# Second chunk through row loads and TensorE transposes, weights requested early, later casts held, rows loaded in pairs

## The chip, the cores and the metric

The kernel runs on one core of a Trainium2 chip. A core has a matrix engine (TensorE, PE in the profile), a vector engine (VectorE, DVE), an activation engine (ScalarE, ACT), a general engine (GpSimd, POOL) and a queue for DMA requests (SyncE, SP). Each of them works through its own instructions in order; they wait for each other through semaphores. The metric is the device time of one execution in microseconds (us).

## The reference

The reference is a short causal convolution followed by a two-layer network with a gated nonlinearity.

```python
# x: (8, 4096, 192), weight: (8 heads, 7 taps); each head has 24 channels
w = softmax(weight, axis=-1)                       # over the 7 taps
x_pad = 6 zero rows ahead of each sequence
out = einsum('hk,bskhg->bshg', w, windows_of_7(x_pad))   # per head, causal
# 32768 tokens of 192 channels; w_in: (192, 2048), w_out: (2048, 192), beta: (2048,)
h = out @ w_in
g = h * sigmoid(beta * h)
y = g @ w_out
```

All inputs and the result are float32; the kernel computes the network in bfloat16 with float32 sums.

## The kernel before, in words

**Tiling.** The eight sequences are folded into two halves, h = 0 and 1, so one chunk is 512 tokens of sequence p and of sequence p + 4 at once; there are 32 chunks. The 192 channels are cut into three groups of 64 (`NG`), so a chunk in transposed form, `xt`, is 128 partitions (half, channel within the group) by three groups by 16 + 512 tokens, the 16 in front being the halo of the tokens before (`HALO`).

**How a chunk is made.** For chunks 1 to 31, `cast(ch)` (line 97) issues two DMAs on POOL's queue, one for each half, that convert the rows to bfloat16 into a tensor `xd` in HBM. `xpose(ch)` (line 110) issues one transposing DMA on SP's queue that brings it into SBUF as `xt`. `conv_ops` (line 336) then makes the convolved chunk `ct` on VectorE, 21 operations for three groups and seven taps, with the softmaxed taps in `cw`. Chunk 0 goes another way, since nothing is there yet: its rows are loaded by SP (line 140), cast by VectorE (line 262), transposed by TensorE (line 270), copied out of PSUM by ScalarE (line 273), and convolved on TensorE with diagonal matrices (`diag_tap`, line 254). Those matrices hold the taps before they are normalized (`eu`), and the sums are scaled by `rn` on the way out (lines 305 and 307). Group 0 of chunk 1 is also convolved on TensorE, in the generator `conv1` (line 326), whose seven steps are spread over u = 4 to 10 of stage 0; it first converts the chunk's group 0 to `xt1` (line 327).

**Weights.** `w_in` is loaded in four quarters of 512 columns and held on both halves of the partitions. The first quarter is loaded twice by SP as float32 and cast by VectorE (lines 145 and 309); the other three are loaded and cast by DMAs on POOL's queue (`load_w_in`) into the lower half and copied to the upper half by VectorE (`copy_w_in`, line 186). `w_out` is loaded in four quarters by SP (`load_w_out`, line 132) and scaled by 1/beta on VectorE (`scale_w_out`, line 291). SP's order before is: the rows of chunk 0, w_in's first quarter, w_out's first quarter, the transpose of chunk 1, then the other w_out quarters.

**The main loop.** Stage s handles chunk s in 16 steps u. A step computes 128 of the 2048 hidden columns for all tokens of the chunk (`hidden`, line 355: six matmuls on 64 rows each, two of them side by side, into one of two PSUM tiles `ph`, then one activation on ScalarE into `g`). Beside it run output pairs (`output`, line 440). An output job covers 256 tokens (one half, two blocks of 128) and needs 32 pairs of matmuls, two for each of the 16 hidden column blocks; a stage has four jobs, so 128 pairs. Two jobs can be under way, in slots a and b, which are the PSUM tiles `pa` and `pb`. A pair can only run on hidden columns that are at least two steps old (`LAG`). `output(s, u, pairs, free)` runs up to `pairs` pairs, the oldest job first, and gives free slots named in `free` to waiting jobs. A job that ends is reduced by VectorE from its PSUM tile (line 412), and SP writes the result out. What is left after the last stage is drained in a closing loop.

**The order written out by hand.** VectorE's convolution operations stand in a queue, from which each step pops some: in stage 0 one or two a step from u = 4 on (16 in all), later 24 a stage. `first_work` gives the steps of stage 0 at which VectorE prepares further quarters of the weights. Every stage issues `cast(s + 4)` at u = 0 and `xpose(s + 2)` at u = 1, where the operations of chunk s + 2 also join the queue. Matmuls of zeros (`fill`, line 211) run between the first small matmuls.

Of the kernel before, what the change touches and what calls it, by code (L numbers as in the profile page):

```python
# [9 lines left out]
FP32 = mybir.dt.float32  # L10
FP32R = mybir.dt.float32r
BF16 = mybir.dt.bfloat16
# [5 lines left out]
def kernel(  # L18
# [17 lines left out]
    nc = tc.nc  # L36

    B, S, D = x.shape
# [3 lines left out]
    DG = 64  # L42
# [41 lines left out]
    def in_b():  # L84
        return psum_b.tile([128, 2, TOK], FP32, name="pb")
# [23 lines left out]

    def xpose(ch):  # L110
        r0 = HALO if ch % CHUNKS == 0 else 0
        xd = xds.pop(ch)
        nc.sync.dma_start_transpose(  # L113
            new_xt(ch)[:, :, r0:], xd[r0:].rearrange("t c h d -> t (c h d)")
        )
# [2 lines left out]
    NW = 4  # L118
    FW = F // NW
    NQ = NF // NW  # L120
    x0 = setup.tile([128, NB, 2, D], FP32)
    x0b = setup.tile([128, NB, NG, 2, DG], BF16)
    w_in_s = consts.tile([128, NG, F], BF16)
    w_in_raw = setup.tile([128, NG, FW], FP32)
    w_out_s = consts.tile([128, NF, D], BF16)
    w_out_raw = setup.tile([128, NF, D], FP32)
    w_in_v = moe_w_in.rearrange("(c d) f -> d c f", c=NG)
# [7 lines left out]
    cw8 = setup.tile([H, K], FP32)  # L135
    beta_q = setup.tile([NF, 128], FP32)
    nc.scalar.dma_start(out=cw8, in_=weight)
    nc.scalar.dma_start(out=beta_q, in_=moe_beta.rearrange("(c p) -> c p", p=128))
    for b in range(NB):
        nc.sync.dma_start(  # L140
            out=x0[:, b, :, :], in_=x_v[0, b * BLK : (b + 1) * BLK, :, :]
        )
    for r in range(2):
        nc.sync.dma_start(
            out=w_in_raw[r * DG : (r + 1) * DG], in_=w_in_v[:, :, 0:FW]
        )
    load_w_out(0)

    zeros = setup.tile([128, TOK], BF16)
    nc.vector.memset(zeros, 0.0)  # L150
# [29 lines left out]
    def load_w_in(i):  # L180
        cols = slice(i * FW, (i + 1) * FW)
        nc.gpsimd.dma_start(out=w_in_s[0:DG, :, cols], in_=w_in_v[:, :, cols])

    def copy_w_in(i):
        cols = slice(i * FW, (i + 1) * FW)
        nc.vector.tensor_copy(w_in_s[DG : 2 * DG, :, cols], w_in_s[0:DG, :, cols])

    cast(1)
    for i in range(1, NW):
        load_w_in(i)  # L190
    cast(2)
    cast(3)
    xpose(1)
    for i in range(1, NW):
        load_w_out(i)

    nmax = setup.tile([H, 1], FP32)
    nc.vector.reduce_max(nmax, cw8, axis=mybir.AxisListType.X, negate=True)
    nc.scalar.activation(
        e8[:, 0:K], cw8, AF.Exp, bias=nmax, accum_out=e8[:, K : K + 1]  # L200
    )
    nc.scalar.activation(warm, warm, AF.Silu)
    sel_r = setup.tile([H, NG, 2, DG], FP32R)
    nc.vector.tensor_copy(sel_r, sel)
# [14 lines left out]
    def spread(dst, sel, e8):  # L219
        for c in range(NG):  # L220
            nc.tensor.matmul(
                dst[:, c * (K + 1) : (c + 1) * (K + 1)],
                sel[:, c, :, :].rearrange("i h d -> i (h d)"),
                e8,
                start=True,
                stop=True,
            )

    fill(5)
    pc = in_a()  # L230
    spread(pc[:, 0, :], sel_r, e8r)
    fill(1, 384)
    eu = setup.tile([128, NG, K + 1], FP32)
    nc.vector.tensor_copy(eu.rearrange("p c k -> p (c k)"), pc[:, 0, 0:NK])

    diag = setup.tile([128, NG, K, 128], FP32R)

# [13 lines left out]
    def new_ct(s):  # L251
        cts[s] = ct_pool.tile([128, NG, TOK], BF16, name="ct")
# [4 lines left out]
            pv, diag[:, c, k, :], xt[:, o : o + TOK], start=(k == 0), stop=(k == K - 1)  # L257
        )


    for b in range(NB):
        nc.vector.tensor_copy(
            x0b[:, b].rearrange("q c h d -> q h c d"),
            x0[:, b].rearrange("q h (c d) -> q h c d", c=NG),
        )
    for b in range(NB):
        pool, name = (psum_b, "pb") if b % 2 == 0 else (psum_a, "pa")
        pt = pool.tile([128, NG, BLK], BF16, name=name)
        for c in range(NG):
            nc.tensor.transpose(  # L270
                pt[:, c, :], x0b[:, b, c].rearrange("q h d -> q (h d)"), ident_b
            )
        nc.scalar.copy(xt0[:, :, HALO + b * BLK : HALO + (b + 1) * BLK], pt)  # L273
        fill(1, 128)
    pb = pf[:, 1, 0:NF]
    nc.tensor.transpose(pb, beta_q, ident[0:NF, 0:NF])
    fill(1)
    diag_v(0)
# [10 lines left out]
    def scale_w_out(i):  # L289
        fcs = slice(i * NQ, (i + 1) * NQ)  # L290
        nc.vector.tensor_tensor(  # L291
            w_out_s[:, fcs, :],
            w_out_raw[:, fcs, :],
            beta_r[:, fcs].unsqueeze(2).to_broadcast((128, NQ, D)),
            ALU.mult,
        )

    new_ct(0)
    for c in range(NG):
        pv = psum_h.tile([128, 2, TOK], FP32, name="ph") if c < 2 else in_a()  # L300
        pv = pv[:, 0, :]
        for k in range(K):
            diag_tap(c, k, xt0[:, c], pv)
        if c < 2:
            nc.vector.tensor_scalar_mul(cts[0][:, c, :], pv, rn[:, c : c + 1])  # L305
# [9 lines left out]
    def taps():  # L315
# [5 lines left out]
        nc.vector.tensor_tensor(  # L321
            cw, pq[:, :, 0:K], rq.unsqueeze(2).to_broadcast((128, NG, K)), ALU.mult
        )


    def conv1():
        nc.vector.tensor_copy(xt1, xts[1][:, 0, :])  # L327
# [112 lines left out]
    def output(s, u, pairs, free):  # L440
        for _ in range(pairs):
            for name in free:
                if slots[name] is None and waiting:
                    slots[name] = waiting.popleft()

            live = [(j.s, j.h, j.q, n) for n, j in slots.items() if j is not None]
            for *_, name in sorted(live):
                job = slots[name]
                if job.ready(s, u):
                    break  # L450
            else:
                return
            if job.po is None:
                job.po = place[name]()
            if job.pair():
                job.leave()
                slots[name] = None

    conv1_work = conv1()
# [75 lines left out]
```

## Time and profile before

| what | us |
|---|---|
| median of ten runs | 719.84 (718.32 to 721.74) |
| the profiled execution, its own time | 718.32 |
| its span, first to last instruction | 716.6 |
| TensorE busy | 695.0 (97%) |
| ScalarE busy | 578.5 (81%) |
| VectorE busy | 522.2 (73%) |
| POOL busy | 60.3 (8%) |

A row of the profile names a line of the kernel, an engine, an operation and its tiles, written out<-in; then come the count, the busy time, the mean of one in ns, and the idle time of the engine just before it with what ended that. `PEld` is the loading of weights into TensorE, which overlaps its matmuls. A `q` behind an engine's name means its queue of requests, not its arithmetic. Rows of the timeline begin with the start and the length in us; several like instructions are merged into one row with their count. Rows of the chain of waits hold start, length, and what the end of the program waited for in that time. In the rows by stretch of time the number after the busy times is the clock that TensorE was granted, as a share of the full one.

### The profile page before, as it was taken

The page shows a single profiled execution, that of the slowest core. Times are in us where ns is not written, and L with a number is a line of the kernel's source. Part 1 is how long each engine was busy: PE and PEld are TensorE (multiplying, and loading weights), DVE is VectorE, ACT ScalarE, POOL GpSimd, SP SyncE. Part 2 cuts the span into 40 slices and gives each one's busy share as a digit, 9 for nine tenths or more (in the row PEclk, how much of TensorE's full clock was granted, in tenths as well). Part 3 has the DMA queues.
Part 4 walks back from the last instruction along what each step waited for, and adds up shares of the span by engine and source line. Part 5 has one row for each costly group of instructions (what it writes and reads, how often), then busy time and mean ns, then how long its engine had stood idle before and what let it go on. Part 6 is the DMA issues. An engine that isn't in the chain of part 4 may idle for free.

```text
span 716.6 us, 24619 instructions
## 1 busy us (share of the span) xinstructions
PE 695.0 (97%) x11325; PEld 521.2 (73%) x11325; DVE 522.2 (73%) x807; ACT 578.5 (81%) x532; POOL 60.3 (8%) x74
## 2 busy tenths in 40 slices
PE   8599999999999999999999999999999999999997
PEld 5267777777777777777777777777777777777776
DVE  5478887988977777977777987667887777797221
ACT  5388888888888888888888888888888888888883
POOL 6374442000000000000000000000000000000000
PEclk9799999999999999999999999999999999999999
DMA  9999999422123222132223122232112322213111
GB/s 184 184 164 165 169 176 171 78 57 60 32 69 69 58 68 57 36 57 68 58 68 59 46 48 69 62 64 57 50 42 70 68 57 59 61 38 63 46 40 52
DMA packets 188088, 55.57 MB, mean 78 GB/s; under 512 B 151168, under 2 KB 187600, under 8 KB 187984
## 3 DMA queue, kind: packets, MB, share of 16 engines
q0 software_dynamic: 99536, 13.13, 28.0%
q1 hardware_dynamic: 88400, 40.86, 24.3%
q8 instruction: 88, 1.44, 0.8%
q14 instruction: 16, 0.13, 0.1%
q10 hardware_dynamic: 48, 0.01, 0.0%
HBM read 29.40 MB, written 37.70 MB: 94 GB/s over the span
## 4 chain that ended last, share of the span: by engine, by line
PE 59%; DVE 24%; DMA 11%; issue 4%; SPq 1%; POOL 0%; ACT 0%; POOLq 0%; DVEq 0%
PE ph L363 28%; PE pa L393 16%; DVE ct L347 16%; PE pb L393 14%; DMA xt<-xd 8%; DVE osb L412 7%; DMA xd<-in_x_dram 2%; DMA w_out_raw<-in_moe_w_out_dram 1%; DVE ct L345 1%; SPq L420 1%; PE pb L256 1%; SPq L113 0%; ACT g L371 0%; POOL xd L104 0%; DVE w_out_s L291 0%
## 5 line engine op out<-in xcount | busy, mean ns | idle before, releaser
L371 ACT ACTIVATE g<-ph,beta 128x1024 bf16<-128x1024 f32 x512 | 570.0, 1114 | 120.6 <-PE ph L363 116.5
L393 PEld LDWEIGHTS <-g 64*128 64x128 bf16 x8192 | 367.8, 94 | 119.2 <-issue 18.5
L363 PE MATMUL ph<-ct,w_in_s 64*128 64x512 bf16 x3072 | 423.8, 377 | 0.3 <-ACT g L371 0.2
L347 DVE SCALAR_TENSOR_TENSOR ct<-xt,cw,ct 128x512 bf16<-128x512 bf16 x552 | 371.8, 748 | 0.0
L393 PE MATMUL pa<-w_out_s,g 64*128 64x192 bf16 x4128 | 240.5, 243 | 7.3 <-DVE osb L412 5.4
L393 PE MATMUL pb<-w_out_s,g 64*128 64x192 bf16 x4064 | 224.5, 243 | 0.0
L363 PEld LDWEIGHTS <-w_in_s 64*128 64x128 bf16 x3072 | 158.3, 94 | 54.0 <-issue 0.9
L345 DVE TENSOR_SCALAR ct<-xt,cw 128x512 bf16<-128x512 bf16 x92 | 27.5, 351 | 117.9 <-DMA xt<-xd 117.9
L412 DVE TENSOR_REDUCE osb<-pa 128x384 f32<-128x768 f32 x64 | 61.1, 955 | 41.2 <-PE pa L393 41.0
L412 DVE TENSOR_REDUCE osb<-pb 128x384 f32<-128x768 f32 x63 | 60.0, 952 | 10.9 <-PE pb L393 10.9
L104 POOL DMA_DIRECT2D xd<-in_x_dram x62 | 56.3, 909 | 53.3 <-DMA xd<-in_x_dram 50.8
L256 PE MATMUL pb<-xt,diag 128*128 128x512 f32 x7 | 4.1, 582 | 8.6 <-DVE xt L327 8.6
L256 PEld LDWEIGHTS pb<-xt,diag 128*128 128x128 f32 x7 | 1.5, 215 | 12.0 <-DVE xt L327 9.0
L291 DVE TENSOR_TENSOR w_out_s<-w_out_raw,beta_r 128x768 bf16<-128x768 f32 x4 | 3.8, 952 | 8.8 <-DMA w_out_raw<-in_moe_w_out_dram 8.8
L213 PE MATMUL ph<-zeros 128*128 128x512 bf16 (+2 forms) x11 | 4.7, 501 | 1.3 <-DVE warm L152 1.3
L256 PE MATMUL ph<-xt,diag 128*128 128x512 f32 x14 | 5.2, 547 | 0.0
L409 ACT COPY osb<-pb 128x192 f32<-128x192 f32 x1 | 0.3, 318 | 5.6 <-DMA out_dram<-osb 5.6
L256 PEld LDWEIGHTS ph<-xt,diag 128*128 128x128 f32 x14 | 3.8, 284 | 1.2 <-ACT xt L273 0.2
L307 ACT ACTIVATE ct<-pa,rn 128x512 bf16<-128x512 f32 x1 | 0.7, 687 | 4.9 <-PE pa L256 4.9
L305 DVE TENSOR_SCALAR ct<-ph,rn 128x512 bf16<-128x512 f32 x2 | 1.5, 746 | 2.3 <-PE ph L256 2.3
L333 DVE TENSOR_SCALAR ct<-pb,rn 128x512 bf16<-128x512 f32 x1 | 0.8, 751 | 3.2 <-PE pb L256 3.2
L213 PEld LDWEIGHTS <-zeros 128*128 128x128 bf16 x11 | 1.4, 136 | 2.1 <-DVE warm L152 1.3
(52 smaller groups left out, 33.5 us busy)
## 6 DMA issues: line engine op xcount, KB each, us to landing
out_dram<-osb SPq DMA_DIRECT2D x127, 192.0 KB, 2.1
xd<-in_x_dram POOLq DMA_DIRECT2D x56, 198.0 KB, 14.9
w_out_raw<-in_moe_w_out_dram SPq DMA_DIRECT2D x4, 384.0 KB, 9.9
xd<-in_x_dram POOLq DMA_DIRECT2D x6, 192.0 KB, 12.1
x<-in_x_dram SPq DMA_DIRECT2D x4, 192.0 KB, 3.2
w_in_raw<-in_moe_w_in_dram SPq DMA_DIRECT2D x2, 384.0 KB, 6.8
w_in_s<-in_moe_w_in_dram POOLq DMA_DIRECT2D x3, 192.0 KB, 11.2
xt<-xd SPq DMA_TRANSPOSE x31, 4.3
```

The lines of the kernel that those rows point to most:

```text
L104: nc.gpsimd.dma_start(out=xd[r0:, :, h, :], in_=x_v[p, t0:t1, h, :].rearrange("t (c d) -> t c d", c=NG),)
L213: nc.tensor.matmul(pf[:, 0, 0:cols], zeros[:, 0:128], zeros[:, 0:cols], start=True, stop=True)
L256: nc.tensor.matmul(pv, diag[:, c, k, :], xt[:, o : o + TOK], start=(k == 0), stop=(k == K - 1))
L291: nc.vector.tensor_tensor(w_out_s[:, fcs, :], w_out_raw[:, fcs, :], beta_r[:, fcs].unsqueeze(2).to_broadcast((128, NQ, D)), ALU.mult,)
L305: nc.vector.tensor_scalar_mul(cts[0][:, c, :], pv, rn[:, c : c + 1])
L345: nc.vector.tensor_scalar_mul(dst, src, scalar)
L347: nc.vector.scalar_tensor_tensor(out=dst, in0=src, scalar=scalar, in1=dst, op0=ALU.mult, op1=ALU.add)
L363: nc.tensor.matmul(ph[:, h, :], w_in_s[rows, j, fc * 128 : (fc + 1) * 128], cts[s][rows, j, :], start=(j == 0), stop=(j == NG - 1),)
L371: nc.scalar.activation(gs[s][:, fc], ph, AF.Silu, scale=beta[:, fc : fc + 1])
L393: nc.tensor.matmul(self.po[:, r, b * D : (b + 1) * D], g[rows, fc, self.h, q * BLK : (q + 1) * BLK], w_out_s[rows, fc, :], start=(self.don ...
L412: nc.vector.tensor_reduce(dst, self.po[:, :, 0 : nb * D].rearrange("p r n -> p n r"), axis=mybir.AxisListType.X, op=ALU.add,)
L420: nc.sync.dma_start(out=out_v[self.h, p, t : t + nb * BLK, :].rearrange("(b q) d -> q b d", q=BLK), in_=osb[:, 0:nb, :],)
```

## The change

Four things are changed, nearly all of them in the start and in stage 0.

1. Chunk 1 no longer goes through POOL's cast and SP's transpose. Its rows are loaded by SP right behind those of chunk 0 (`load_x`), cast on VectorE (`cast_rows`, during the convolution of chunk 0), transposed on TensorE and copied out of PSUM by VectorE, in a new generator `second` that runs in u = 1 to 3 of stage 0. Its last step also makes the taps `cw`, as `taps` did before.
2. SP requests both chunks' rows and then all four quarters of w_out ahead of everything else. All four quarters of w_in come by POOL's queue, the first at once and the others after a one-element copy on POOL (`hold`) that waits for `eu`. The casts of chunks 2 and 3 come after a second such copy, which waits for the last tokens of the transposed chunk 1.
3. Rows are loaded two tokens in a row for each partition, so that a DMA covers 256 tokens with runs of 1536 bytes. A block of 128 rows then holds every second token, and the copies out of PSUM put the tokens back in order (`tokens`, and the rearranged views in `second`).
4. Stage 0 gives out output pairs in another number (3 a step in u = 3 to 10, 5 in u = 11 to 15), and the transposes of later chunks are issued one stage earlier (`xpose(s + 3)`), while their convolution operations join the queue at u = 4.

```diff
-    x0 = setup.tile([128, NB, 2, D], FP32)
+    x0 = setup.tile([128, 2, 2, 2, D], FP32)
+    x1 = setup.tile([128, 2, 2, 2, D], FP32)
     x0b = setup.tile([128, NB, NG, 2, DG], BF16)
+    x1b = setup.tile([128, NB, NG, 2, DG], BF16)
-    w_in_raw = setup.tile([128, NG, FW], FP32)
...
     nc.scalar.dma_start(out=cw8, in_=weight)
-    nc.scalar.dma_start(out=beta_q, in_=moe_beta.rearrange("(c p) -> c p", p=128))
-    for b in range(NB):
-        nc.sync.dma_start(
-            out=x0[:, b, :, :], in_=x_v[0, b * BLK : (b + 1) * BLK, :, :]
-        )
-    for r in range(2):
-        nc.sync.dma_start(
-            out=w_in_raw[r * DG : (r + 1) * DG], in_=w_in_v[:, :, 0:FW]
-        )
-    load_w_out(0)
+
+    def load_x(dst, t0):
+        for i in range(2):
+            t = t0 + i * 2 * BLK
+            nc.sync.dma_start(
+                out=dst[:, i].rearrange("q h b d -> q h (b d)"),
+                in_=x_v[0, t : t + 2 * BLK, :, :].rearrange(
+                    "(q b) h d -> q h (b d)", b=2
+                ),
+            )
+
+    load_x(x0, 0)
+    load_x(x1, TOK)
+    for i in range(NW):
+        load_w_out(i)
...
-    cast(1)
-    for i in range(1, NW):
-        load_w_in(i)
-    cast(2)
-    cast(3)
-    xpose(1)
-    for i in range(1, NW):
-        load_w_out(i)
+    load_w_in(0)
...
+    nc.scalar.dma_start(out=beta_q, in_=moe_beta.rearrange("(c p) -> c p", p=128))
...
     fill(5)
     pc = in_a()
-    spread(pc[:, 0, :], sel_r, e8r)
-    fill(1, 384)
+    for c in range(NG):
+        spread(pc[:, 0, :], sel_r, e8r, c)
+        fill(1, 256)
+    for b in range(NB):
+        cast_rows(x0b, x0, b)
     eu = setup.tile([128, NG, K + 1], FP32)
     nc.vector.tensor_copy(eu.rearrange("p c k -> p (c k)"), pc[:, 0, 0:NK])
+    hold = setup.tile([1, 2], FP32)
+    nc.gpsimd.tensor_copy(hold[:, 0:1], eu[0:1, 0, 0:1])
+    for i in range(1, NW):
+        load_w_in(i)
...
     for b in range(NB):
-        pool, name = (psum_b, "pb") if b % 2 == 0 else (psum_a, "pa")
-        pt = pool.tile([128, NG, BLK], BF16, name=name)
...
-        nc.scalar.copy(xt0[:, :, HALO + b * BLK : HALO + (b + 1) * BLK], pt)
+        pt = pts[b % 2][:, b // 2, 0 : NG * BLK].rearrange("p (c q) -> p c q", c=NG)
+        transposes(pt, x0b, b)
+        nc.scalar.copy(tokens(xt0, b), pt)
         fill(1, 128)
...
+    copy_w_in(0)
     new_ct(0)
...
         if c == 0:
-            nc.vector.tensor_copy(w_in_s[:, :, 0:FW], w_in_raw)
-    scale_w_out(0)
+            for b in range(NB):
+                cast_rows(x1b, x1, b)
...
+    def second():
+        xt = new_xt(1)
+        pt = in_b()
...
+        for i in range(2):
+            for b in range(2):
+                transposes(halves[i][:, :, b], x1b, 2 * i + b)
+            t = HALO + i * 2 * BLK
+            nc.vector.tensor_copy(
+                xt[:, :, t : t + 2 * BLK].rearrange("p c (q b) -> p c q b", b=2),
+                halves[i].rearrange("p c b q -> p c q b"),
+            )
+            if i == 0:
+                nc.vector.tensor_copy(
+                    xt[:, :, HALO - PAD : HALO], xt0[:, :, HALO + TOK - PAD :]
+                )
+                scale_w_out(0)
+            yield
+        nc.gpsimd.tensor_copy(hold[:, 1:2], xt[0:1, 0, HALO + TOK - 1 :])
+        cast(2)
+        cast(3)
         pq = in_b()[:, 0, 0:NK]
-        spread(pq, sel, e8)
+        for c in range(NG):
+            spread(pq, sel, e8, c)
         pq = pq.rearrange("p (c k) -> p c k", c=NG)
+        copy_w_in(1)
         rq = setup.tile([128, NG], FP32)
...
+        yield
...
     first_work = {
-        1: lambda: (copy_w_in(1), scale_w_out(1)),
+        4: lambda: scale_w_out(1),
...
-            else:
-                taps()
+            if s == 0 and 0 < u < 4:
+                next(second_work)
             if s == 0 and u in CONV1:
                 next(conv1_work)
-            output(s, u, 8, "a" if s == 0 and u <= CONV1[-1] else "ab")
+            if s > 0:
+                output(s, u, 8, "ab")
+            elif u > CONV1[-1]:
+                output(s, u, 5, "ab")
+            elif u > 2:
+                output(s, u, 3, "a")
...
-            if u == 0 and s + 4 < N_CH:
+            if u == 0 and s > 0 and s + 4 < N_CH:
                 cast(s + 4)
-            if u == 1 and s + 2 < N_CH:
-                xpose(s + 2)
+            if u == 1 and s > 0 and s + 3 < N_CH:
+                xpose(s + 3)
+            if s == 0 and u == 4:
+                xpose(2)
+                cast(4)
+            if s == 0 and u == 12:
+                xpose(3)
+            if u == 4 and s + 2 < N_CH:
                 queue.extend(conv_ops(s + 2, 0))
```

More of the change, by code (lines that the diff above doesn't have):

```diff
@@ L217, with spread, cast_rows, transposes @@
     NK = NG * (K + 1)
-    def spread(dst, sel, e8):
-        for c in range(NG):
[L221 to L226, printed above, removed]
-            )
+    def spread(dst, sel, e8, c):
+        nc.tensor.matmul(
+            dst[:, c * (K + 1) : (c + 1) * (K + 1)],
+            sel[:, c, :, :].rearrange("i h d -> i (h d)"),
+            e8,
+            start=True,
+            stop=True,
+        )
+    def cast_rows(xb, x, b):
+        nc.vector.tensor_copy(
+            xb[:, b].rearrange("q c h d -> q h c d"),
+            x[:, b // 2, :, b % 2].rearrange("q h (c d) -> q h c d", c=NG),
+        )
+    def transposes(pt, xb, b):
+        for c in range(NG):
+            nc.tensor.transpose(
+                pt[:, c, :], xb[:, b, c].rearrange("q h d -> q (h d)"), ident_b
+            )
+    def tokens(xt, b):
+        t = HALO + (b // 2) * 2 * BLK
+        return xt[:, :, t : t + 2 * BLK].rearrange("p c (q b) -> p c b q", b=2)[:, :, b % 2]
     fill(5)
     pc = in_a()
-    spread(pc[:, 0, :], sel_r, e8r)
-    fill(1, 384)
+    for c in range(NG):
[3 more added lines that the diff above has]
+        cast_rows(x0b, x0, b)
     eu = setup.tile([128, NG, K + 1], FP32)
     nc.vector.tensor_copy(eu.rearrange("p c k -> p (c k)"), pc[:, 0, 0:NK])
+    hold = setup.tile([1, 2], FP32)
+    nc.gpsimd.tensor_copy(hold[:, 0:1], eu[0:1, 0, 0:1])
+    for i in range(1, NW):
+        load_w_in(i)
     diag = setup.tile([128, NG, K, 128], FP32R)
@@ L258, in diag_tap @@
         )
+    pts = [
+        pool.tile([128, 2, 2 * TOK], BF16, name=name)
+        for pool, name in ((psum_b, "pb"), (psum_h, "ph"))
+    ]
     for b in range(NB):
[L262 to L266, printed above, removed]
-        pool, name = (psum_b, "pb") if b % 2 == 0 else (psum_a, "pa")
-        pt = pool.tile([128, NG, BLK], BF16, name=name)
[L269 to L272, printed above, removed]
-        nc.scalar.copy(xt0[:, :, HALO + b * BLK : HALO + (b + 1) * BLK], pt)
+        pt = pts[b % 2][:, b // 2, 0 : NG * BLK].rearrange("p (c q) -> p c q", c=NG)
+        transposes(pt, x0b, b)
+        nc.scalar.copy(tokens(xt0, b), pt)
         fill(1, 128)
-    pb = pf[:, 1, 0:NF]
+    pb = pc[:, 1, 0:NF]
     nc.tensor.transpose(pb, beta_q, ident[0:NF, 0:NF])
@@ L308 @@
         if c == 0:
-            nc.vector.tensor_copy(w_in_s[:, :, 0:FW], w_in_raw)
-    scale_w_out(0)
+            for b in range(NB):
+                cast_rows(x1b, x1, b)
     cw = consts.tile([128, NG, K], FP32)
-    def taps():
+    def second():
+        xt = new_xt(1)
+        pt = in_b()
+        halves = [
+            pt[:, i, 0 : NG * BLK].bitcast(BF16).rearrange(
+                "p (c b q) -> p c b q", c=NG, b=2
+            )
+            for i in range(2)
+        ]
+        for i in range(2):
[5 more added lines that the diff above has]
+                halves[i].rearrange("p c b q -> p c q b"),
+            )
+            if i == 0:
+                nc.vector.tensor_copy(
+                    xt[:, :, HALO - PAD : HALO], xt0[:, :, HALO + TOK - PAD :]
+                )
+                scale_w_out(0)
[3 more added lines that the diff above has]
+        cast(3)
         pq = in_b()[:, 0, 0:NK]
-        spread(pq, sel, e8)
+        for c in range(NG):
+            spread(pq, sel, e8, c)
         pq = pq.rearrange("p (c k) -> p c k", c=NG)
+        copy_w_in(1)
         rq = setup.tile([128, NG], FP32)
@@ L323, in taps @@
         )
+        yield
     def conv1():
-        nc.vector.tensor_copy(xt1, xts[1][:, 0, :])
+        nc.vector.tensor_copy(
+            xt1[:, HALO - PAD :], xts[1][:, 0, HALO - PAD :]
+        )
         new_ct(1)
@@ L457, in output @@
                 slots[name] = None
+    second_work = second()
     conv1_work = conv1()
     first_work = {
-        1: lambda: (copy_w_in(1), scale_w_out(1)),
+        4: lambda: scale_w_out(1),
         5: lambda: copy_w_in(2),
```

## The prediction, before the result was known

> **What bounds the kernel now.** I read the page's totals, the waits, the chain of work that ended last, then the rows around each place that the chain names.
>
> ```profile
> span 716.6 us, 24619 instructions
> PE 695.0 (97%) x11325; PEld 521.2 (73%) x11325; DVE 522.2 (73%) x807; ACT 578.5 (81%) x532; POOL 60.3 (8%) x74
> ```
> ```profile
> DVE ct L345 <- DMA xt<-xd: 117.9, 26, 5.5
> ```
> ```profile
> PE pb L256 <- DVE xt L327: 8.6, 1, 8.6
> ```
>
> TensorE sets the time, so what counts is its own waiting. It waits once for 8.6 us, at the first tap of chunk 1's convolution. VectorE's 117.9 us of waits for transposed chunks are on an engine with slack. The chain, and two VectorE rows, show why the long wait is there:
>
> ```profile
> 3.97 10.89 DMA xd<-in_x_dram
> 14.89 0.05 issue
> 14.94 2.96 SPq L113
> 17.89 0.05 issue
> 17.94 9.23 DMA w_out_raw<-in_moe_w_out_dram
> ```
> ```profile
> 27.20 0.96 DVE L291 TENSOR_TENSOR w_out_s<-w_out_raw,beta_r 128x768 bf16<-128x768 f32 x1 [8.79 <-DMA w_out_raw<-in_moe_w_out_dram]
> 28.08 0.43 DVE L327 CAST xt<-xt 128x528 fp32r<-128x528 bf16 x1
> ```
>
> SP issues in order. The request for w_out's second quarter stands behind the transpose of chunk 1, which waits for that chunk's cast; it goes out at 17.94, lands at 27.2, and VectorE, in order too, holds the cast of xt1 (L327) behind the scaling of that quarter. The idle also costs clock afterwards (columns: stretch, length, busy times, granted clock, DMA share, GB/s):
>
> ```profile
> 28.56:34.18 5.62, 5.62 (x34) 2.27 (x34) 5.49 (x10) 2.23 (x2) 0.95 (x1) 0.68 1.64 176
> 34.18:38.22 4.04, 4.04 (x35) 1.68 (x33) 1.37 (x2) 3.34 (x3) 2.95 (x4) 1.00 2.44 155
> ```
>
> Three steps u take 5.62 at clock 0.68 and 4.04 at 1.00: 1.6 us more. The second loss comes at each change of stage. The first one, and the last with a piece of the stage that follows, in the chain:
>
> ```profile
> 45.36 0.65 PE ph L363 x6
> 46.01 0.43 PE pa L393 x8
> 46.46 0.97 DVE osb L412
> 47.43 0.04 issue
> 47.47 0.84 PE pa L393 x16
> ```
> ```profile
> 686.47 0.83 PE pa L393 x16
> 687.30 0.65 PE ph L363 x6
> ...
> 692.53 0.65 PE ph L363 x6
> ```
>
> From 47.47 to 686.47 are 30 stages: 639.0, or 21.30 each. A step without a change takes (692.53 - 687.30)/4 = 1.3075, and sixteen take 20.92. So 0.38 us of each stage is lost, where the chain leaves TensorE for the reduction L412.
>
> **Why both result banks end together.** In stage 0 the kernel before does 2 output pairs in each of u = 2 to 10 (slot a alone, two per new column), 8 in u = 11 to 14 and 6 in u = 15: 56 of 128. Each later stage does 128, so 72 are carried over every time: 4 + 4 + 32 + 32. At u = 0 slots a and b lack 4 pairs each, both end there, and the third job needs bank a while its reduction (0.97) runs beside only 4 pairs and one hidden step.
>
> The change does 3 and 3 pairs, then 2 six times (u = 3 to 10: 18), and 5 in each of u = 11 to 15: 43. Carried over are 85 = 4 + 17 + 32 + 32. Slot a ends at u = 0, slot b 17 pairs later at u = 2, the next ones at u = 6 and u = 10, in every stage alike. Bank a then has 17 pairs (1.4 us) and two hidden steps (1.3), 2.7 us, for its reduction:
>
> ```profile
> L412 DVE TENSOR_REDUCE osb<-pa 128x384 f32<-128x768 f32 x64 | 61.1, 955 | 41.2 <-PE pa L393 41.0
> ```
>
> VectorE mostly waits for TensorE ahead of these (41.2 us), so it is on time. Also, the chunk transposes move a stage earlier (s + 3 at u = 1), which removes the 117.9 us of waits; those now push taps late into a stage, where they can delay a reduction. I take the whole loss away: 30 x 0.38 = 11.4, about 0.2 for the change at 47, and 0.7 in the drain:
>
> ```profile
> 707.55 2.82 PE L393 MATMUL pa<-w_out_s,g 64*128 64x192 bf16 x64 [0.72 <-DVE osb L412]
> ```
>
> Together **-12.3**. The other end is 0, if reductions came over 2.7 us after the last pair.
>
> **Fewer pairs early, more at the end.** Thirteen pairs move from stage 0 into the drain. Before, u = 11 to 15 took four steps of 1.31 and one with 6 pairs (1.14): 6.37. With 5 pairs TensorE needs 0.65 + 0.41 a step, less than ScalarE's 1.125 from the row below, so five steps take 5.6: -0.75. In the drain a pair takes 2.82/32 = 0.088: +1.1. Sum **+0.35**; were the early steps no shorter, +1.1.
>
> ```profile
> 44.91 2.25 ACT L371 ACTIVATE g<-ph,beta 128x1024 bf16<-128x1024 f32 x2 [0.20 <-PE ph L363]
> ```
>
> **The first 21 us.** Rows of the head: the loads of x0 and their casts, VectorE, TensorE.
>
> ```profile
> L140 SPq DMA_DIRECT2D x<-in_x_dram x4: 453/466/472, 0.8 to 2.3; - x4
> L262 DVE CAST x0b<-x x4: 305/350/508, 5.0 to 6.2; 128x384 bf16<-128x384 f32 x4
> ...
> DMA to landing us min/median/max: 2.6/3.2/3.9
> ```
> ```profile
> 11.29 0.75 DVE L305 TENSOR_SCALAR ct<-ph,rn 128x512 bf16<-128x512 f32 x1 [2.25 <-PE ph L256]
> ...
> 17.18 0.18 DVE L321 TENSOR_TENSOR cw<-pb,rq 128x21 f32<-128x21 f32 x1
> 17.39 1.02 DVE L186 COPY w_in_s<-w_in_s 64x1536 bf16<-64x1536 bf16 x1
> ```
> ```profile
> 7.89 5.24 PE L256 MATMUL ph<-xt,diag 128*128 128x512 f32 x14
> 12.98 1.79 PE L256 MATMUL pa<-xt,diag 128*128 128x512 f32 x7
> 14.70 1.47 PE L363 MATMUL ph<-ct,w_in_s 64*128 64x512 bf16 x12
> 16.10 0.83 PE L221 MATMUL pb<-e,sel 8*128 8x8 f32 x6
> ```
>
> x0 landed at 2.3 + 3.9 = 6.2. The same 768 KB now come in two requests without chunk 1's casts beside them; I put the last landing at about 5.3 (an estimate; bounds 4.9, a start at 2.3 with the shortest landing of 2.6, and 6.2). The strided write of transposed tokens keeps its price (doubled, it would cost the head about half a us). Convolution then starts near 7.4, not 7.89. Its first 14 taps take 5.24, the last 7 only 1.79, so the rate steps up on the way; if that step stays at its place in time, the half us is worth 0.3 and the hidden layer starts at 14.4, not 14.70. Before that VectorE has, in order, the copy of w_in's first quarter (1.02), ct (0.75), four casts of x1 (1.4), ct (0.75): with the first ct at 10.8 it ends at 13.7, in time.
>
> From 14.4: twelve matmuls to 15.7, six transposes to 16.2 (six times 128 columns, 0.4 at the rate of the last taps, 0.8 at that of the first). The copies out of PSUM aren't in the trace; the nearest rows are L412 (768 elements, 0.96) and two casts of 384 (0.7); I take 0.96. VectorE: copy to 17.25, halo and scaling of w_out's first quarter to 18.3, second copy to 19.25, w_in's second quarter to 20.25. The three small matmuls need the same PSUM tile: 19.3 to 20.1. Reciprocal and taps, 0.18 each, to 20.6, xt1 (0.43) to 21.0, tap 0 at **21.1 in place of 28.56: -7.5**. The added TensorE work hides under ScalarE, whose 1.125 a step paces u = 1 to 3. The idle stretch gone, the clock stays: **-1.6**.
>
> **Weights.** Due are w_in's first quarter by 10 us (then it begins to hold ct), x1 by 11.5, w_out's quarters by 17, 21, 25 and 30. SP has issued everything by about 6 and nothing waits ahead of it; the later w_in quarters follow the hold on eu, near 6. All together is some 3.9 MB: 22 to 25 us at the 176 and 155 GB/s of the rows above, in order of need, so in time. Only w_in's first quarter is open. Before, its queue gave
>
> ```profile
> DMA to landing us min/median/max: 10.9/11.2/11.6
> ```
>
> From an issue at 3.0 that would be 14.2, and ct at 14.2 + 1.02 + 0.75 + 1.4 + 0.75 = 18.1, 3.7 late. But those quarters stood behind two casts of x, and this one stands first in its queue: I take 0. The Trainium skill, "DMA: Bandwidth & Descriptors" (Queues, rings and completion order), says that each DMA engine serves its queue rows in turn, packet by packet. By that rule w_in's quarter would share with x and land early, and the sum would be the same; by the row alone it would be 3.7 more.
>
> **The held casts.** Casts of chunks 2 and 3 now wait on POOL for chunk 1's last copy (19.25), and cast 4 and all later ones stand behind them. SP's transpose of chunk 2 waits for its cast. Transposes, then casts, of the first 60 us, from issue to landing:
>
> ```profile
> DMA to landing us min/median/max: 9.6/11.3/13.0
> ```
> ```profile
> DMA to landing us min/median/max: 9.6/14.6/19.6
> ```
>
> Chunk 2's first taps pop at u = 15, near 35; blocked taps hold the reduction of slot a, and TensorE misses it from about 37.5. Two casts issued by 21.1 land 3.2 (as x did) to 9.6 later, the transpose 11 after that: 35 to 42, so 0 to 4.3 us. I take **+0.5**, as the cast queue is empty then.
>
> **Sum**, against the profiled execution's own 718.32 (span 716.6 and 1.7 around it): -7.5 - 1.6 + 0.35 - 12.3 + 0.5 = -20.5, or 697.8. That execution is the quickest of the ten, 1.5 under their median of 719.84; part of their spread should be the uneven stage changes, which go. I forecast **698**.
>
> **Rivals.**
> *The stage change keeps its loss*: taps crowd VectorE, and reductions come late. Then 718.3 - 7.5 - 1.6 + 0.35 + 0.5 = 710. For it: VectorE is busy 73% over all. Against: its 41.2 us of waiting ahead of L412.
> *Late data in the head*: w_in's quarter (up to +3.7) or chunk 2 (up to +4.3): 701 to 706.
> *The clock steps up earlier*, as fills now stand between the first small matmuls. Some eight taps at 0.26 (1.79/7) in place of over 0.37 (5.24/14) would save 1 to 1.5: 696.5. The Trainium skill, "TensorE: Matmul & The Clock Gate" (Part 1: The HAM clock gate), says that activity is judged over free-running windows of about 3.4 us. By that rule the step moves by a whole window or not at all; the 0.68 after the idle agrees that the clock follows activity.
> *Slower, by the held casts.* The place is chunk 2's first tap at u = 15, the price one us of TensorE per us that the chunk lands after 37.5, and the kernel is slower from a landing near 58 on. The slowest cast and transpose of the rows above give 21.1 + 19.6 + 13.0 = 53.7, or 714; so even the worst rows stop short of it, and they had weights in their way.
> *No change*: the early requests do nothing and stage changes stay. The chain's order speaks against it.
>
> **Chances.** Forecast 0.60 (its own range 695.5 to 701); stage change kept, wholly or in part, 0.17; late data 0.13; early clock 0.05; slower 0.03; no change 0.02. The range 694 to 710 leaves out the last two and the outer ends. Differences under 0.2% (1.4 us) can't be told from none. Faster 0.95, same 0.02, slower 0.03.
>
> **What would show it.** Right: chunk 1's first tap near 21 with no long idle ahead, clock 1.00 from 12 on, stages of 20.9, no two reductions back to back, hardly a VectorE wait for xt, a drain of 85 pairs. Wrong: VectorE waiting for w_in or x1 before 14 or for xt between 35 and 42, or stages still near 21.3.

## The result, and the profile after

The changed kernel takes 697.11 us (median of 9 runs, 696.17 to 697.38; a tenth on record took 697.66) against 719.48 for the kernel before (32 runs); the ratio is 0.968, 95% interval 0.967 to 0.970. The forecast was 698. The profiled execution took 696.75, with a span of 695.0. Its totals, and then everything that TensorE still waits for (who waits, for whom: total us, times, longest):

```profile
span 695.0 us, 24650 instructions
PE 688.1 (99%) x11339; PEld 497.7 (72%) x11339; DVE 527.6 (76%) x814; ACT 578.0 (83%) x532; POOL 61.3 (9%) x75
```
```profile
PE ph L213 <- DVE warm L158: 1.3, 1, 1.3
PE ph L411 <- ACT g L419: 0.6, 1, 0.6
PE pa L441 <- ACT g L419: 0.4, 1, 0.4
PE pb L220 <- DVE xt L346: 0.3, 1, 0.3
PE pa L293 <- DMA beta_q<-in_moe_beta_dram: 0.2, 1, 0.2
```

The 8.6 us wait is gone and so is every wait for a reduction (L460, formerly L412). In VectorE's waits nothing stands for transposed chunks any more; it waits for TensorE instead:

```profile
DVE osb L460 <- PE pa L441: 121.9, 61, 6.8
```

The chain of work after, from the small matmuls that make the taps to the change from stage 0 to 1, and its last stage with the drain (start, length, what):

```profile
18.63 0.83 PE pb L220 x6
...
20.46 0.43 PE pb L279
...
29.32 0.65 PE ph L411 x6
...
34.62 0.65 PE ph L411 x6
35.26 0.49 PE pa L441 x8
35.75 0.33 PE pb L441 x8
36.08 0.65 PE ph L411 x6
```
```profile
663.68 0.65 PE ph L411 x6
...
681.99 0.67 PE ph L411 x6
```

The chain stays on TensorE from 18.63 to the drain. At the change, 8 matmuls on bank a end its job, 8 on bank b follow, and the next hidden step comes at once. From 36.08 to 663.68 are 30 stages of 20.92, the number worked out for a stage without loss. The same places in the chain of before, where they weren't shown yet:

```profile
38.99 0.65 PE ph L363 x6
```
```profile
704.30 0.66 PE ph L363 x6
```

| stretch | before | after | gain | forecast |
|---|---|---|---|---|
| start to chunk 1's first tap | 28.56 | 20.46 | 8.1 | 7.5 |
| from there to step 11 | 10.43 | 8.86 | 1.6 | 1.6 |
| steps 11 to 15 of stage 0 | 6.37 | 5.30 | 1.1 | 0.75 |
| stages 1 to 31, to the last hidden step | 658.94 | 647.37 | 11.6 | 11.6 |
| drain, to the end of the span | 12.3 | 13.0 | -0.7 | -0.4 |
| late chunk 2 | | none | 0 | -0.5 |
| sum | 716.6 | 695.0 | 21.6 | 20.5 |

### The profile page after: what moved, and what is told of

Its sections match the earlier page's. It is cut to its first block, busy times and chain, and to the rows that moved or that the text cites. A ratio compares the mean times of both kernels' runs of the same rounds, so it can differ in the third digit from the quotient of the medians.

```text
span 695.0 us, 24650 instructions
## 1 busy us (share of the span) xinstructions
PE 688.1 (99%) x11339; PEld 497.7 (72%) x11339; DVE 527.6 (76%) x814; ACT 578.0 (83%) x532; POOL 61.3 (9%) x75
## 4 chain that ended last, share of the span: by engine, by line
PE 98%; DMA 1%; ACT 0%; DVE 0%; issue 0%; ACTq 0%
PE ph L411 48%; PE pa L441 25%; PE pb L441 24%; DMA beta_q<-in_moe_beta_dram 1%; PE ph L279 1%; PE pb L279 0%; PE pa L279 0%; ACT g L419 0%; DVE xt L346 0%; ACT L159 0%; DVE w_out_s L308 0%; PE pb L220 0%; ACTq L138 0%; PE ph L213 0%; PE pb L237 0%
## 5 line engine op out<-in xcount | busy, mean ns | idle before, releaser
L441 PEld LDWEIGHTS <-g 64*128 64x128 bf16 x8192 | 352.3, 94 | 121.2 <-issue 1.7
L411 PE MATMUL ph<-ct,w_in_s 64*128 64x512 bf16 x3072 | 415.1, 376 | 0.6 <-ACT g L419 0.6
L395 DVE SCALAR_TENSOR_TENSOR ct<-xt,cw,ct 128x512 bf16<-128x512 bf16 x552 | 376.0, 746 | 0.0
L441 PE MATMUL pa<-w_out_s,g 64*128 64x192 bf16 x4128 | 234.1, 243 | 0.4 <-ACT g L419 0.4
L411 PEld LDWEIGHTS <-w_in_s 64*128 64x128 bf16 x3072 | 141.9, 94 | 62.0 <-issue 0.9
L460 DVE TENSOR_REDUCE osb<-pa 128x384 f32<-128x768 f32 x64 | 61.3, 958 | 122.3 <-PE pa L441 121.9
L460 DVE TENSOR_REDUCE osb<-pb 128x384 f32<-128x768 f32 x63 | 60.1, 954 | 31.6 <-PE pb L441 31.6
L393 DVE TENSOR_SCALAR ct<-xt,cw 128x512 bf16<-128x512 bf16 x92 | 29.8, 356 | 0.0
L192 DVE COPY w_in_s<-w_in_s 64x1536 bf16<-64x1536 bf16 x4 | 3.0, 760 | 1.8 <-DMA w_in_s<-in_moe_w_in_dram 1.7
L346 DVE COPY xt<-pb 128x768 bf16<-128x768 bf16 x2 | 1.9, 958 | 2.2 <-PE pb L237 2.2
```

The lines of the kernel that those rows point to most:

```text
L346: nc.vector.tensor_copy(xt[:, :, t : t + 2 * BLK].rearrange("p c (q b) -> p c q b", b=2), halves[i].rearrange("p c b q -> p c q b"),)
L393: nc.vector.tensor_scalar_mul(dst, src, scalar)
L395: nc.vector.scalar_tensor_tensor(out=dst, in0=src, scalar=scalar, in1=dst, op0=ALU.mult, op1=ALU.add)
L411: nc.tensor.matmul(ph[:, h, :], w_in_s[rows, j, fc * 128 : (fc + 1) * 128], cts[s][rows, j, :], start=(j == 0), stop=(j == NG - 1),)
L441: nc.tensor.matmul(self.po[:, r, b * D : (b + 1) * D], g[rows, fc, self.h, q * BLK : (q + 1) * BLK], w_out_s[rows, fc, :], start=(self.don ...
L460: nc.vector.tensor_reduce(dst, self.po[:, :, 0 : nb * D].rearrange("p r n -> p n r"), axis=mybir.AxisListType.X, op=ALU.add,)
```

## The experiments

The stated times are medians; the kernel before ran beside each group on the same chip (720.2 to 720.6).

**1. The output pairs alone, in the kernel before.**

```diff
-            output(s, u, 8, "a" if s == 0 and u <= CONV1[-1] else "ab")
+            output(s, u, 5 if s == 0 and u > CONV1[-1] else 8, "a" if ... else "ab")
```

> The kernel before, with one number changed: stage 0 gives out 5 output pairs, not 8, in u = 11 to 15, so 85 pairs are carried over and slot b ends 17 pairs after slot a. Theory (the order in which the two result banks end is the whole stage-change loss): stages fall from 21.30 to about 20.9, no TensorE wait on L412, 719.5 - 12.3 + 0.4 = 707.5 us. Rival 1 (the uneven part of the loss, about 4 us, comes from transposes that land late and push taps ahead of a reduction, and it stays): about 711.5. Rival 2 (the loss has another cause): 719.5. The 8.6 us wait in stage 0 stays by all of them.

Measured: 707.07 us, ratio 0.982 (0.980 to 0.984). The longest of its TensorE waits, and the first change of stage in its chain:

```profile
PE pb L256 <- DVE xt L327: 9.0, 1, 9.0
```
```profile
45.72 0.49 PE pa L393 x8
46.21 0.33 PE pb L393 x8
```

The early wait is still there. Among the others, of 1.3 us and less, none is for L412 any more. VectorE still waits 65.3 us in all for late transposes in this kernel, and TensorE hardly feels it. One number moves 13 us.

**2. The other way round: the changed kernel with 8 pairs again.**

```diff
             elif u > CONV1[-1]:
-                output(s, u, 5, "ab")
+                output(s, u, 8, "ab")
```

> The changed kernel with that one number put back: 8 pairs in u = 11 to 15, so 72 are carried over and both slots end together at u = 0. Theory: each of 31 changes costs the undisturbed 0.24 again (7.5 us), the drain its 0.7, less 0.4 of shorter drain and stage: 697.1 + 7.8 = about 705; the uneven part does not come back, since transposes are a stage early. Rival (the uneven part belongs to the two reductions and the taps in one queue, however early the transposes are): about 709.

Measured: 706.03, ratio 0.981 (0.978 to 0.983). Its chain at the first two changes:

```profile
37.37 0.97 DVE osb L460
38.34 0.04 issue
38.38 0.84 PE pa L441 x16
...
58.54 0.97 DVE osb L460
59.50 0.04 issue
59.55 0.84 PE pa L441 x16
```

The chain leaves TensorE for the reduction again, and 59.55 - 38.38 is 21.17: a loss of 0.25 against 20.92 at this change and at all the later ones alike. This is the undisturbed loss, with VectorE on time. The uneven part (3.9 us: the 639.0 of before less 30 x 21.17) does not come back.

The trace of before shows where that part came from. At its even changes of stage the reduction of bank a starts 0.27 us after ScalarE's first activation of the new stage, and the stage takes 21.17, from that activation to the next stage's. At the change of 471.70 the reduction starts 0.74 after it, with no idle ahead: VectorE had waited 5.37 us for a chunk and was still at the taps behind it (rows of VectorE, then of TensorE, in the kernel before):

```profile
457.99 0.88 DVE L345 TENSOR_SCALAR ct<-xt,cw 128x512 bf16<-128x512 bf16 x3 [5.37 <-DMA xt<-xd]
...
472.44 0.96 DVE L412 TENSOR_REDUCE osb<-pa 128x384 f32<-128x768 f32 x1
```
```profile
473.45 0.75 PE L393 MATMUL pa<-w_out_s,g 64*128 64x192 bf16 x14 [0.54 <-DVE osb L412]
```

That stage took 21.63, longer than 21.17 by the 0.47 that the reduction was late. Eleven changes of before are late in this way, by 0.04 to 0.58 us, and at each the stage is longer by the same amount within 0.01. So the uneven part had two cures, each enough: experiment 1 removes it by slack, this kernel by early transposes. That shows in the sums too: 13.2 (experiment 1) and 14.2 (this one), both against the kernel before that ran beside them, are 27.4 together, some 4 more than the 23 of the whole change.

**3. Transposes as late as before, the shift kept.**

```diff
-            if u == 1 and s > 0 and s + 3 < N_CH:
-                xpose(s + 3)
+            if u == 1 and s > 1 and s + 2 < N_CH:
+                xpose(s + 2)
```

> The changed kernel with the chunk transposes issued as late as before (chunk s + 2 at u = 1 of stage s); the shifted slots stay. Theory (2.7 us of slack at the one tight reduction cover taps that come late): VectorE waits for xt again, 50 to 100 us in all, and the time stays within 1 us of 697.1. Rival (early transposes carry the uneven part of the gain): about 701, with TensorE waiting on L460.

Measured: 699.25 (698.18 to 699.31), 2.1 above the changed kernel, between the two expectations. The waits for late chunks were 44.7 us. TensorE paid in one place, in the chain near 133 us:

```profile
121.88 10.67 DMA xt<-xd
...
133.19 0.87 DVE osb L460
```

A chunk landed at 132.6, with VectorE blocked at its taps and the reduction of bank a behind them; by its TensorE waits this cost 0.6 and 0.3 us of idle, and two stages came out 1.5 longer together. VectorE had waited 5.7 us for this chunk and at most 2.4 for any other: the slack covers the ordinary lateness, not this one. The rest lies, in this execution, in the head (first tap at 21.3, not 20.4, see experiment 7), which the edit does not touch.

**4. The weights alone, in the kernel before.**

```diff
-    xpose(1)
     for i in range(1, NW):
         load_w_out(i)
+    xpose(1)
```

> The kernel before, with the three later w_out quarters requested ahead of the transpose of chunk 1; nothing else. Theory (the queue order explains only the last piece of the long wait; behind it stands the transposed chunk itself, cast on POOL and transposed through SP): w_out no longer ends the wait, the first tap of chunk 1 comes near 25 and not 28.6, the idle is still over 4 us and still costs clock: 719.5 - 3 = about 716.5. Rival 1 (w_out's place in the queue is the whole of it): first tap near 21, 710. Rival 2 (the transpose, now behind 1.2 MB of weights, lands as late as w_out did): no change.

Measured: 721.22, ratio 1.001 (1.000 to 1.003): no change. VectorE's rows around the wait:

```profile
20.50 0.96 DVE L291 TENSOR_TENSOR w_out_s<-w_out_raw,beta_r 128x768 bf16<-128x768 f32 x1
28.70 0.43 DVE L327 CAST xt<-xt 128x528 fp32r<-128x528 bf16 x1 [7.24 <-DMA xt<-xd]
```

The scaling of w_out's second quarter no longer waits, at 20.50, and the first tap is no sooner: the transposed chunk itself lands at 28.7. Its way there in this kernel's chain, and the issue of the same transpose in the kernel before, with its time to landing:

```profile
3.97 14.15 DMA xd<-in_x_dram
...
18.19 10.48 DMA xt<-xd
```
```profile
xt<-xd SPq DMA_TRANSPOSE x1, 9.6
```

Before, the transpose went out at 14.94 and landed 9.6 later, at 24.5, so w_out, which the chain named, held chunk 1 up for the last 2.7 us of the wait and no longer. With the weights requested ahead, the cast takes 14.15 in place of 10.89 and the transpose 10.48, and the chunk lands 4.2 later than before. The second rival of the expectation is what happened: early weights alone take away one wait and lengthen the other. What they would be worth if they did not hold up the chunk, at most those 2.7, this experiment can't tell.

**5. The second hold taken away.**

```diff
     for i in range(1, NW):
         load_w_in(i)
+    cast(2)
+    cast(3)
...
-        nc.gpsimd.tensor_copy(hold[:, 1:2], xt[0:1, 0, HALO + TOK - 1 :])
-        cast(2)
-        cast(3)
```

> The changed kernel without the second hold: the casts of chunks 2 and 3 are requested right behind the later w_in quarters, at about 9 us instead of 19. Theory (the weights and chunk 1 are requested ahead of them, so the hold buys little): chunk 2 lands some 8 us sooner, w_out's later quarters some us later but before they are due, the time within 1 us of 697.1. Rival (the hold is what keeps chunk 1 and the weights early): VectorE waits for w_in's second or w_out's second quarter in u = 3 to 5, 700 or more.

Measured: 697.58 (697.14 to 698.19), ratio 0.970 (0.967 to 0.972). No difference that can be told; there is no wait for w_out, and the transpose of chunk 2 goes out 5 us sooner (8 were expected) for nothing:

```profile
20.32 8.16 SPq L113 DMA_TRANSPOSE xt<-xd  x2
```

In the changed kernel this row starts at 25.16. Holding these casts neither helps nor harms.

**6. How far apart the banks must end.** Two kernels with other numbers of pairs in the last steps of stage 0, the first with seven pairs between the ends of the two banks, the second with five.

```diff
-                output(s, u, 5, "ab")
+                output(s, u, 7, "ab")
```

> The changed kernel with 7 pairs in u = 11 to 15: 75 carried over, slot b ends 7 pairs after slot a. A reduction then has 7 pairs (0.58) and one hidden step (0.65), 1.23 us; with 4 pairs (0.98) the loss was 0.24 in each stage, so it needs 1.22. Theory (loss = what is lacking from 1.22, plus VectorE's lateness): stages of 20.92 or a few hundredths more, 697 to 698. Rival (any closeness of the two ends costs, since both reductions queue on VectorE): stages of 21.0 or more, 700.

```diff
-                output(s, u, 5, "ab")
+                output(s, u, 8 if u < NF - 1 else 5, "ab")
```

> The changed kernel with 8 pairs in u = 11 to 14 and 5 in u = 15: 73 carried over, slot b ends 5 pairs after slot a. Theory (a reduction needs 1.22 us; 5 pairs and one hidden step are 0.41 + 0.65 = 1.06): each of 31 stage changes costs 0.16, stages of 21.08, about 697.1 + 5 + 0.6 in the drain - 0.4 = 702.3. Rival (the loss is all or nothing, by the order in which the reductions queue): 21.17 as with both ends together, 706, or 20.92, 697.

Measured: 697.31 with seven pairs (0.969, 0.967 to 0.971), 702.95 with five (0.976, 0.974 to 0.978). The chain of the kernel with five, at two changes:

```profile
36.68 0.33 PE pb L441 x8
37.02 0.65 PE ph L411 x6
37.66 0.08 PE pb L441 x2
37.74 0.75 PE pa L441 x14
...
58.10 0.65 PE ph L411 x6
```

58.10 - 37.02 is 21.08, which is 20.92 + 0.16 as worked out. Four pairs cost 0.25 a stage, five 0.16, seven and seventeen nothing. The loss is the missing time itself: a bank must rest about 1.2 us, of which the reduction is 0.96. Seventeen pairs and two hidden steps are 2.7 us, so 1.5 to spare, and the two reductions that came later than that show it: 1.63 late in experiment 1 and 1.77 in experiment 3, with stages longer by 0.14 and 0.29. In the chain above no reduction appears at all, as the ends of matmuls are modelled; the loss sits unseen in the 0.75 of 14 matmuls (elsewhere in that chain 14 take 0.58).

**7. VectorE's copy of w_in's first quarter behind the casts of x1.**

```diff
-    copy_w_in(0)
     new_ct(0)
...
             for b in range(NB):
                 cast_rows(x1b, x1, b)
+            copy_w_in(0)
```

> The changed kernel with VectorE's copy of w_in's first quarter moved behind the first ct and the casts of x1. In the runs so far that quarter landed at 10.4 to 11.7 and held the first ct on VectorE; where the clock stepped up early, TensorE then waited 0.7 to 1.3 us for the second ct. Theory (late w_in in front of ct is a cost of the head): the copy no longer waits, the hidden layer starts without a gap, 696 to 696.6. Rival (the second ct, now behind the copy, is as late): no change, 697.1.

Measured: 697.37 (696.77 to 697.44), ratio 0.969 (0.967 to 0.971): no difference. The profile can't decide the cause, because the TensorE rate stepped up late in this execution. The 14 first taps, by kernel (the kernel of experiment 3, experiment 1, the changed kernel, this one):

```profile
7.87 3.89 PE L279 MATMUL ph<-xt,diag 128*128 128x512 f32 x14
```
```profile
7.90 4.59 PE L256 MATMUL ph<-xt,diag 128*128 128x512 f32 x14
```
```profile
7.87 4.42 PE L279 MATMUL ph<-xt,diag 128*128 128x512 f32 x14
```
```profile
7.88 5.02 PE L279 MATMUL ph<-xt,diag 128*128 128x512 f32 x14
```

They start within 0.03 us of each other and take 3.9 to 5.0 us (5.24 in the profile of before). Of these four the rate stepped up soonest in experiment 3, and there w_in's quarter, which landed at 11.7, was the limit:

```profile
11.76 0.69 DVE L192 COPY w_in_s<-w_in_s 64x1536 bf16<-64x1536 bf16 x1 [3.19 <-DMA w_in_s<-in_moe_w_in_dram]
```
```profile
15.01 1.26 PE L411 MATMUL ph<-ct,w_in_s 64*128 64x512 bf16 x10 [1.30 <-DVE ct L323]
```

Whether the later copy gains in such an execution stays open; over its runs it doesn't.

**8. Rows one token at a time.**

```diff
-            nc.sync.dma_start(out=dst[:, i].rearrange("q h b d -> q h (b d)"),
-                in_=x_v[0, t : t + 2 * BLK, :, :].rearrange("(q b) h d -> q h (b d)", b=2))
+            for b in range(2):
+                nc.sync.dma_start(out=dst[:, i, :, b],
+                    in_=x_v[0, t : t + 2 * BLK, :, :].rearrange("(q b) h d -> b q h d", b=2)[b])
```

> The changed kernel with each row load of 256 tokens split into two requests that take every second token, so runs of 768 bytes, not 1536, at the same places; all else equal. Theory (the convolution starts when ScalarE has copied the last block, and the loads have little slack there): x0 lands up to 0.5 us later, x1 up to 1, and the time rises by 0 to 1 us. Rival 1 (run length makes no difference): equal landings, 697.1. Rival 2 (short runs hold up x1 and with it the hidden layer): 699 or more.

Measured: 697.20 (696.10 to 697.93), ratio 0.969 (0.967 to 0.972). The convolution begins at 7.95, not 7.87, and the hidden layer at 13.82, not 13.85. The rows do land later (those of x0 by 6.2 and not 5.5, those of x1 by 10.9 and not 8.9), and it costs nothing here, so loading them in pairs bought nothing.

**9. Chunk 1's TensorE taps in twos.**

```diff
             if k == K - 1:
                 nc.vector.tensor_scalar_mul(cts[1][:, 0, :], pv, rn[:, 0:1])
-            yield
+            if k % 2 == 1 or k == K - 1:
+                yield
...
-            if s == 0 and u in CONV1:
+            if s == 0 and 4 <= u < 8:
                 next(conv1_work)
```

> The changed kernel with the seven taps of chunk 1's group 0 given out in twos, in u = 4 to 7 instead of one a step in u = 4 to 10. A tap alone takes 0.42 on TensorE's chain, one in a row of taps 0.235. Theory (the switch between full and half array is paid per visit): three visits fewer, 0.5 to 0.6 us less, 696.6, if ScalarE at 1.07 a step does not become the bound in u = 8 to 10. Rival (ScalarE takes it back): no change.

Measured: 697.93 (697.34 to 698.17), ratio 0.969 (0.967 to 0.971): no gain, if anything a loss. The rows of TensorE at the beginning of stage 1:

```profile
33.91 0.40 PE L412 MATMUL ph<-ct,w_in_s 64*128 64x512 bf16 x2
35.01 0.39 PE L412 MATMUL ph<-ct,w_in_s 64*128 64x512 bf16 x2 [0.71 <-DVE ct L396]
```

Stage 1 begins at 33.91, half a us sooner than in the changed kernel (34.45). Of that, 0.2 was there at the first tap already (20.16, not 20.39), so the taps in twos gained 0.3 on TensorE. Then stage 1 waits for chunk 1's taps on VectorE, 1.0 us in two pieces, the larger of them in the second row. The edit itself put VectorE behind. Its copy of the finished tap sums, in this kernel and then in the changed one:

```profile
25.52 0.75 DVE L381 TENSOR_SCALAR ct<-pb,rn 128x512 bf16<-128x512 f32 x1 [1.54 <-PE pb L279]
```
```profile
29.08 0.75 DVE L381 TENSOR_SCALAR ct<-pb,rn 128x512 bf16<-128x512 f32 x1 [0.51 <-PE pb L279]
```

The copy comes three steps earlier, VectorE waits 1.54 us for TensorE there in place of 0.51, and all of its own taps behind it come later. Whether the 0.3 could be kept with the copy left at its place, no run shows.

## Why the prediction was right, point by point

**The stage change** was right in its mechanism, its place and its size: 11.6 us of stages, forecast 11.6, with 20.92 a stage as worked out from one clean step. Experiments 1, 2 and 6 show it from both sides and with a slope. Counting the pairs carried over (72 before, 85 after), not reading waits, found it. The list of waits of before showed less than half of the loss:

```profile
PE pa L393 <- DVE osb L412: 5.4, 11, 0.7
```

Ten of these eleven waits stand at the late changes and one in the drain; the even 0.25 of each change shows as no idle time at all. The reason given for the irregular part, late transposes that push taps against a reduction, is shown by the late reductions of before and by experiment 2, where that part is gone with the banks back together. Early transposes and the shift each suffice, so neither has a share of its own.

**The first 21 us** came out near (20.4 for 21.1), in part by luck: two steps of the working failed, and a gain came that the change does not bring. Convolution was to start at 7.4, since x0 lands sooner. It did land sooner (at 5.5, not 6.2), by the casts that waited for its second half:

```profile
5.48 0.63 DVE L230 CAST x0b<-x 128x384 bf16<-128x384 f32 x2 [0.42 <-DMA x<-in_x_dram]
```

But the convolution began at 7.87, and at 7.89 before: between them stand four transposes and some matmuls of zeros at the low rate and four copies on ScalarE, which take the time whenever the rows come. What moved the hidden layer to 13.85 (14.4 was forecast) is the TensorE rate. By the spacing of the taps, 0.43 us and then 0.23, it stepped up near 9.7 in this execution and near 11.7 in the profile of before, and the 14 taps took 4.42, not 5.24. The change didn't bring that: the kernel of experiment 1 has the head of before, and its 14 taps took 4.59. From the hidden layer to the first tap it took 6.5 us, 6.7 in the forecast, so that part of the working held.

The price of w_in's first quarter was taken as 0. It took 7.5 us from its issue:

```profile
10.43 0.69 DVE L192 COPY w_in_s<-w_in_s 64x1536 bf16<-64x1536 bf16 x1 [1.67 <-DMA w_in_s<-in_moe_w_in_dram]
```

That is past the 10 us at which it was due, and VectorE stood for 1.67. Here it cost nothing, as the sums for the first ct were ready only shortly before and the hidden layer followed the taps at once; in experiment 3, where the quarter landed 1.3 later, it cost 1.3. The rule of the Trainium skill that the prediction set beside it, "DMA: Bandwidth & Descriptors" (Queues, rings and completion order), that queue rows are served in turn, would have it land early. It landed after all of x (four requests, issued by 2.3, of at most 6.6), so the rule alone doesn't give a landing time.

**The reading of the first wait** is right for its end only. The prediction called SP's order the cause, with VectorE held behind the scaling of w_out. Both are in the trace, but chunk 1 itself was not there before 24.5, 2.7 us ahead of w_out (experiment 4); the rest of the wait was the cast and the transpose. Requesting the weights early, alone, made these two slower and gained nothing. The gain comes with the other way for chunk 1, by rows and TensorE, which takes casting and transposing DMAs out of its path; no run has that other way with the weights late, so the early weights have no price of their own.

**Smaller terms.** The clock term came out as forecast, 1.6. Steps 11 to 15 took 1.06 each, not 1.125: ScalarE's activations follow one another at 1.07 when nothing stands between. The drain came out 0.3 worse. The 0.5 for held casts was not needed; the transpose of chunk 2 went out at 25.16 and landed at 34.4, only just ahead of its first tap (34.59). In the kernel of experiment 7 it came later and VectorE waited 0.71 us for it, without a wait of TensorE behind it. Experiment 5 shows that the hold doesn't matter either way. The forecast against the median held probably because the irregular part went: the runs of before spread over 5 us (717.7 to 723.1), those of the changed kernel over 1.5. Experiments 1 and 2, without that part, spread over 0.8 and 1.5, experiment 4, with it, over 4.5 (ten runs against four each).

**The rivals.** A kept stage loss would have shown as stages of 21.3; they are 20.92. Late data was half right, as a wait on VectorE and not as a loss. The earlier clock step happened by itself and saved 0.8 in this execution, where 1 to 1.5 had been worked out; the Trainium skill's "TensorE: Matmul & The Clock Gate" (Part 1: The HAM clock gate) says that its windows run free of the kernel, and the equal starts with taps of 3.9 to 5.2 us agree with that. What the prediction drew from that page, a whole window or not at all, did not hold: the step moved by some 1.9 us.

## What to carry to other kernels

Where two accumulators are filled in turn, count at which step each one ends: if both end together, the engine that empties them is on the path once a round, even if it is idle a quarter of the time, and a few units of work moved at the start shift all rounds apart. When a chain names the last arrival, ask what would have come next: here another transfer had landed only 2.7 us earlier, and the requests that were moved ahead of it made it 4.2 later, so that removing the named wait alone changed nothing. Measure how long a bank must rest (here 1.2 us for a reduction of 0.96) before paying for more, and keep some slack beyond it where the reducing engine can be late. Measure periods as well as gaps: the 0.25 us that every stage lost showed in no wait.

## What the runs showed of the hardware that was not expected

The moment at which TensorE's rate steps up in the head differs between executions by more than a us with the same instructions ahead of it. In two kernels with the same head the taps' spacing changed from 0.43 to 0.23 us near 10.3 and near 11.7 (14 taps from the same start: 4.59 and 5.24). A quarter of w_in, first in its own queue, needed 7.5 us to land beside the loads of x and w_out on another queue, and the three behind it as long:

```profile
DMA to landing us min/median/max: 7.4/7.8/8.6
```

Loads with runs of 768 bytes in place of 1536 landed 0.7 us later for x0 and 2.0 for x1, in twice as many requests, and the whole kernel took the same time.
